# Attention followed by a SwiGLU feed-forward on one core: the first batch in a new order, other slots for the scores, no transposes in bare steps

## The chip, the cores and the metric

The kernel runs on one core of a Trainium2 chip. The metric is the device time of one execution in microseconds (us). Before the change the median of three runs is 423.39 us (423.31 to 423.66).

The engines of the core work at the same time, each through its own instructions in the order in which the program gives them: TensorE (PE: matmuls and transposes into PSUM; PEld is its loading of stationary operands), VectorE (DVE), ScalarE (ACT), GpSimd (POOL) and SyncE (SP, which here only issues DMAs). An instruction that waits holds up all that stands behind it on its engine. POOL issues DMAs too, those that change the type from fp32 to bf16 on the way among them.

## The reference

Eight batches, eight heads, 576 positions, head size 64. The attention has a causal mask and a decay that grows with the running sum of `max(s, 0)`:

```python
scores = scale * np.matmul(q, k.transpose(0, 1, 3, 2))
cum = np.cumsum(np.maximum(s, 0.0), axis=-1)
bias = -(cum[:, :, :, None] - cum[:, :, None, :])
scores = np.where(causal, -1000000000.0, scores + np.minimum(bias, 0.0))
attn = softmax(scores)                  # max subtracted, 1e-09 in the denominator
attn_out = np.matmul(attn, v)           # (8, 8, 576, 64)
x = attn_out.transpose(0, 2, 1, 3).reshape(4608, 512)
xn = x / rms(x) * rms_g
g = xn @ w_gate                         # 512 -> 1536
out = (g * sigmoid(g) * (xn @ w_val)) @ w_out
```

## The kernel before, in words

**The feed-forward is the frame.** The 4608 rows of x are cut into nine chunks of 512. `ffn(c)` does one chunk: for each of 12 blocks `fb` of the hidden size, four matmuls for the gate (line 482, called G here), four for the value (line 491, V), a tanh on ACT (485), two products on DVE (494 and 487); then 4 x 12 matmuls with `w_out` (line 506, O), four copies on ACT (511) and four stores by SP. `need(c)` comes before it and has to see that the rows of chunk c are there.

**The attention fills the frame.** After every group of four matmuls `ffn` calls `step()`, which counts a slot and puts a small piece of attention work into the program: 36 slots for each chunk. Its pieces are

- T (`t_step`, line 149): four transposes of k (w = 0) or q (w = 1) for one pair of heads, PSUM to `kqT` by ACT (161) or DVE (159); `tail_step` (163) for the last 64 positions.
- S (`s_step`, 188): for four heads and a block `kb` of 128 keys, score matmuls (203) into a pair of PSUM banks, four exps on ACT (219), and the causal mask by POOL (`affine_select`, 225). Half of the exps and the mask come one slot later (`pending`). In the frame the pair is always `psS`, of which there is one.
- AV (`av_step`, 233): E times V for four heads and 128 queries (240, 246), reciprocal and product on DVE (253, 255). With the second group of heads come a sum of squares on ACT (260) and the root on POOL (263, 266).
- `x_scale` (DVE, 273), XT (`xt_step`, 277: transposes on PE, 281, and a copy on DVE, 286, to `xnT`, which G and V read), `check_mag` and `check_max` (DVE), casts of k and q to bf16 (`cast`, 139 on POOL or DVE, 137 on ACT) and loads of V (`load_v`, 144, POOL).

Which piece a slot takes is fixed when the program is built, by rules in slots: S may follow S after three slots, or after two once the slot number has reached `due`:

```python
due = SLOTS * ((b * S + kb * 128) // DM) - 14
if slot[0] - last["S"] < (3 if slot[0] < due else 2):
```

XT may come six slots after the second AV of its block, `x_scale` three after it, T two slots after the last T or XT. `need(c)` calls `step()` with no matmuls of the frame around it while the last XT of its chunk is missing: bare steps. In the kernel before these are four ahead of chunk 1 and one ahead of chunk 2.

**The first batch comes ahead of the frame** and its order is written out by hand (lines 620 to 676), with `piece` for the casts and `s_first` for S. k and q of batch 0 come through SP in parts, k and q of batch 1 by four DMAs on POOL, and POOL also has the weights: `load_w` loads half of `w_gate` or `w_val` (`wg_sb`, `wv_sb`). All DMAs of POOL go through one queue (q0), those of SP through another (q1).

**PSUM** is eight banks: four in a ring named F (`psF`, `psF16`, `pairF` takes two), two for `psS`, one named AV (`psAV`, `psAV16`) and one named T (`psT`, `psT32`). In the frame F holds G, V and O.

Of the kernel before, what the change touches and what calls it, by code (L numbers as in the profile page):

```python
# [26 lines left out]
def kernel(  # L27
# [12 lines left out]
    nc = tc.nc  # L40
    B, H, S, D = q.shape
    DM = H * D
# [55 lines left out]
    def psF16():  # L98
        return pp.tile([128, 8, 128], BF16, name="psF16", tag="F", bufs=4)
# [7 lines left out]
    def psAV16():  # L107
        return pp.tile([128, 8, 128], BF16, name="psAV16", tag="AV", bufs=1)

    def psT():  # L110
        return pp.tile([128, 8, 128], BF16, name="psT", tag="T", bufs=1)
# [29 lines left out]
    def load_v(b, c):  # L141
        n = rows(c)
        done["V", b, c] = slot[0]
        nc.gpsimd.dma_start(  # L144
            out=v_sb[0:n, b % 2, c, :, 0:64],
            in_=v[b, :, c * 128:c * 128 + n, :].rearrange("h p d -> p h d"))
# [207 lines left out]
    def do_t(key, **kw):  # L354
        b, hp, w = key
        if hp == "tail":
            tail_step(b)
            done["T", b] = slot[0]
            after_tail(b)
        else:  # L360
            if b == 1 and (hp + w) % 2:
                kw["pT"] = psAV16()
            t_step(b, hp, w, **kw)
        done["T", b, hp, w] = slot[0]
        last["T"] = slot[0]
# [24 lines left out]
    def can_t():  # L390
        if not t_seq:
            return False
        b, hp, w = t_seq[0]
        if slot[0] - last["T"] < (1 if b == 1 else 2):
            return False
        return ready(2, "cast", b) and (b < 2 or ready(1, "S", b - 2, 4, 0))

    def can_s():
        if not s_seq or not slot_free():
            return False  # L400
        b, kb, g = s_seq[0]
        due = SLOTS * ((b * S + kb * 128) // DM) - 14
        if slot[0] - last["S"] < (3 if slot[0] < due else 2):
            return False
        if kb >= 3 and not ready(3, "T", b):
            return False
        if kb == 4:
            return True
        return all(ready(3, "T", b, 2 * g + j, w) for j in (0, 1) for w in (0, 1))
# [20 lines left out]
    scaled = [0]  # L430
    x_list = [(b, qb) for b in range(B) for qb in range(NSC)]

    def step():

        slot[0] += 1
        while pending:
            pending.pop(0)()
        if scaled[0] < len(x_list):
            b, qb = x_list[scaled[0]]
            if ready(3, "AV", b, qb, 1):  # L440
                x_scale(b, qb)
                scaled[0] += 1
        if v_side and (slot[0] % 2 or slot[0] < 9):
            run_side(v_side)
        else:
            run_side(pool_side)
        if slot[0] % 2:
            run_side(dve_side)
        if can_s():
            pending.append(do_s(s_seq.pop(0)))  # L450
            return
        n = 0
        if can_xt():
            do_xt(xt_seq.pop(0))
            n += 1
        if can_av():
            do_av(av_seq.pop(0))
            n += 1
        if n < 2 and can_t():
            do_t(t_seq.pop(0))  # L460

    def need(c):

        lastt = (c + 1) * DM - 1
        key = (lastt // S, (lastt % S) // 128)
        n = 0
        while at("XT", *key) > slot[0]:
            step()
            n += 1
            assert n < 200, key  # L470

# [44 lines left out]
    def load_w(src, dst, i):  # L516
        fs = slice(i * (DF // 2), (i + 1) * (DF // 2))
        nc.gpsimd.dma_start(out=dst[:, :, fs],
                            in_=src[:, fs].rearrange("(cc p) f -> p cc f", p=128))
# [62 lines left out]
    with tc.manual_schedule():  # L582

        nc.scalar.dma_start(out=s_sb, in_=s.rearrange("b h s -> (b h) s"))
        for g in (0, 1):
            for w in (0, 1):
                load_kq(nc.sync, 0, w, 4 * g, 4 * g + 4)
        nc.vector.memset(kq32[64:128, :, :, 256:320], 0.0)
        for w in (0, 1):
            load_kq_tail(nc.sync, 0, w)  # L590
        nc.sync.dma_start(out=g_row, in_=moe_rms_g.rearrange("(o d) -> o d", o=1).to_broadcast([128, DM]))
        make_identity(nc, ident_bf)
        make_identity(nc, ident_f)
        nc.gpsimd.memset(shf[:, 4, 64:128], 0.0)
        nc.gpsimd.memset(v_sb[:, 0, :, :, 64:65], 1.0)
        nc.gpsimd.memset(E[:, 6:8, :, 192:256], 0.0)
        nc.vector.memset(mhalf, -0.5)
        nc.vector.memset(stat, 0.0)
        nc.vector.memset(ss_all, 0.0)
        nc.vector.memset(acc, 0.0)  # L600
        nc.vector.memset(kqT[:, :, :, :, 576:640], 0.0)

        s_seq[:] = [x for x in s_seq if x[0] > 0 or x[1] == 4]
        av_seq[:] = [x for x in av_seq if x[0] > 0 or x[1] == 4]
        xt_seq[:] = [x for x in xt_seq if x[0] > 0 or x[1] == 4]
        t_seq[:] = [x for x in t_seq if x[0] > 0]
        scaled[0] = 4

        def piece(w, g, engines):
            for r, eng in enumerate(engines):  # L610
                cast(eng, 0, w, r, r + 1, 4 * g, 4 * g + 4)

        def pairF():
            return (psF(), psF())

        def s_first(kb, g, pair=None):
            return do_s((0, kb, g), pair)

        ACT, DVE, POOL = nc.scalar, nc.vector, nc.gpsimd
        piece(0, 0, (ACT, ACT, ACT, POOL))  # L620
        piece(1, 0, (ACT, ACT, POOL, POOL))
        load_v(0, 0)
        load_v(0, 1)
        do_t((0, 0, 0), pT=psT(), dve=False)
        do_t((0, 1, 0), pT=psF16(), dve=False)
        decay_setup()
        do_t((0, 0, 1), pT=psAV16(), dve=True)
        do_t((0, 1, 1), pT=psF16(), dve=True)
        s_first(0, 0)()
        piece(0, 1, (DVE, DVE, POOL, POOL))  # L630
        load_w(moe_w_gate, wg_sb, 0)
        piece(1, 1, (DVE, DVE, POOL, POOL))
        s_first(1, 0, pairF())()
        do_t((0, 2, 0), pT=psT(), dve=True)
        do_t((0, 3, 0), pT=psAV16(), dve=True)
        do_t((0, 2, 1), pT=psT(), dve=True)
        do_t((0, 3, 1), pT=psAV16(), dve=True)
        load_v(0, 2)
        s_first(0, 1, pairF())()
        s_first(1, 1)()  # L640
        load_w(moe_w_val, wv_sb, 0)
        do_av((0, 0, 0))
        do_av((0, 0, 1), psF())
        for w in (0, 1):
            cast(POOL, 0, w, 4, 5)
        s_first(2, 0, pairF())()
        tail_step(0)
        done["T", 0] = 0
        x_scale(0, 0)
        do_av((0, 1, 0))  # L650
        do_av((0, 1, 1), psF())
        load_v(0, 3)
        s_first(2, 1)()
        do_xt((0, 0))
        s_first(3, 0, pairF())()
        x_scale(0, 1)
        for w in (0, 1):
            load_kq(nc.gpsimd, 1, w)
            load_kq_tail(nc.gpsimd, 1, w)
        do_av((0, 2, 0))  # L660
        do_av((0, 2, 1), psF())
        s_first(3, 1)()
        do_xt((0, 1))
        x_scale(0, 2)
        do_av((0, 3, 0))
        do_av((0, 3, 1), psF())
        load_w(moe_w_gate, wg_sb, 1)
        load_w(moe_w_val, wv_sb, 1)
        do_xt((0, 2))
        nc.gpsimd.memset(v_sb[64:128, :, 4, :, 0:64], 0.0)  # L670
        nc.gpsimd.memset(v_sb[:, 1, :, :, 64:65], 1.0)
        x_scale(0, 3)
        check_mag(0, 0)
        check_mag(0, 1)
        done["check", 0] = 0
        do_xt((0, 3))
        for r in range(NSC):
            cast(ACT, 1, 0, r, r + 1)
            cast(POOL, 1, 1, r, r + 1)
        done["cast", 1] = -20  # L680
        for w in (0, 1):
            load_kq(nc.sync, 2, w)
            load_kq_tail(nc.sync, 2, w)
        done["raw", 2] = 5
        after_tail(0)
        later(v_side, 0, [
            lambda: load_v(0, 4), lambda: load_v(1, 0), lambda: load_v(1, 1),
            lambda: nc.gpsimd.dma_start(out=wout_sb,
                                        in_=moe_w_out.rearrange("(fc p) d -> p fc d", p=128)),
            lambda: load_v(1, 2), lambda: load_v(1, 3), lambda: load_v(1, 4)])  # L690
        check(0, True)
        check(1)

        def extra(fb):
            if fb == 8:
                decay_range()

        for c in range(NCH):
            need(c)
            ffn(c, extra if c == 0 else None)  # L700
            if c == B - 1:
                verdict()
# [185 lines left out]
```

## Time and profile before

| | us |
|---|---|
| median of three runs | 423.39 |
| the profiled execution | 423.98 |
| its span in the profile (first to last instruction) | 422.1 |
| first matmul of chunk 0 | 43.27 |
| first matmul of chunk 1 | 101.07 |

| engine | busy us | share of the span |
|---|---|---|
| PE | 373.4 | 88% |
| DVE | 300.1 | 71% |
| ACT | 242.0 | 57% |
| POOL | 174.9 | 41% |

How to read it: busy time of PE is a pipelined time and not a measure of speed by itself; "PEclk" is the clock that was granted to PE as a share of the full one. In the chain of waits, "A <- B: total, times, longest" says how long A stood idle until B released it. In the timeline a line has its start, its time, its engine, the line of the kernel, what was written from what, and in brackets the idle time before it with what ended it.

### The profile page before, as it was taken

What the parts mean: (1) busy time and instruction counts of PE and PEld (TensorE: products, weight loads), DVE (VectorE), ACT (ScalarE), POOL (GpSimd) and SP (SyncE); (2) the same over time, 40 slices, a digit from 0 to 9 for tenths busy, and PEclk for the clock granted to TensorE, in tenths of its full rate; (3) what the DMA queues carried; (4) which work ended last, traced back from release to release, by engine and by line L of the source; (5) the groups of instructions that cost most, each with busy time, mean ns of one, the idle gap of its engine ahead of it and who ended that gap; (6) DMA issues with size and microseconds to landing.
All of it is one profiled execution on the core that took longest, in us unless ns stands there. A gap on an engine that the chain in (4) does not pass through costs nothing. (4 is left out here: it accounts for less than half of the span.)

```text
span 422.1 us, 7394 instructions
## 1 busy us (share of the span) xinstructions
PE 373.4 (88%) x2679; PEld 182.6 (43%) x2679; DVE 300.1 (71%) x582; ACT 242.0 (57%) x600; POOL 174.9 (41%) x288
## 2 busy tenths in 40 slices
PE   2543888895998989999999999999999999999993
PEld 2222443353444444455444444544454445444441
DVE  5434678866798788887796888787757856774840
ACT  3565455772567758664867585758665873323321
POOL 5457736747417539635633582343220431000000
PEclk9999999896999999999999999999999999999999
DMA  8979999486930837729331630290020011001002
GB/s 236 121 94 233 215 232 174 26 240 107 156 103 1 242 90 51 222 81 82 113 114 75 64 20 0 77 79 5 10 91 2 0 52 52 0 26 76 0 28 80
DMA packets 69244, 38.71 MB, mean 92 GB/s; under 512 B 45904, under 2 KB 63824, under 8 KB 69200
## 3 DMA queue, kind: packets, MB, share of 16 engines
q0 software_dynamic: 41808, 11.80, 28.2%
q1 hardware_dynamic: 27312, 26.22, 20.7%
q8 instruction: 23, 0.38, 0.4%
q14 instruction: 21, 0.17, 0.1%
q10 hardware_dynamic: 80, 0.15, 0.1%
HBM read 38.16 MB, written 9.44 MB: 113 GB/s over the span
## 5 line engine op out<-in xcount | busy, mean ns | idle before, releaser
L219 ACT ACTIVATE E<-psS,biasK 128x256 bf16<-128x256 f32 (+2 forms) x304 | 106.8, 435 | 16.5 <-PE psS L203 16.4
L482 PE MATMUL psF<-xnT,wg_sb 128*128 128x512 bf16 x432 | 113.8, 387 | 2.7 <-DVE xnT L286 2.5
L491 PE MATMUL psF<-xnT,wv_sb 128*128 128x512 bf16 x432 | 113.7, 386 | 0.9 <-DVE Ht L487 0.9
L506 PE MATMUL psF<-wout_sb,Ht 128*128 128x512 bf16 x432 | 105.0, 380 | 0.0
L485 ACT ACTIVATE T<-psF 128x512 f32<-128x512 f32 x108 | 64.7, 599 | 60.9 <-PE psF L482 54.0
L225 POOL TENSOR_SCALAR_AFFINE_SELECT E<-E 128x512 bf16<-128x512 bf16 x72 | 54.0, 750 | 102.9 <-ACT E L219 102.7
L494 DVE SCALAR_TENSOR_TENSOR U<-T,psF 128x512 bf16<-128x512 f32 x108 | 73.8, 683 | 26.8 <-ACT T L485 26.2
L487 DVE TENSOR_TENSOR Ht<-U,psF 128x512 bf16<-128x512 bf16 x99 | 67.6, 682 | 5.5
L491 PEld LDWEIGHTS <-wv_sb 128*128 128x128 bf16 x432 | 39.4, 99 | 44.5 <-issue 7.5
L482 PEld LDWEIGHTS <-wg_sb 128*128 128x128 bf16 x432 | 38.7, 99 | 40.9 <-issue 10.1
L506 PEld LDWEIGHTS <-Ht 128*128 128x128 bf16 x432 | 37.7, 98 | 38.0 <-issue 2.8
L260 ACT ACTIVATE xs_sb<-x_sb 128x512 bf16<-128x512 bf16 (+1 forms) x40 | 25.2, 631 | 48.3 <-DVE x_sb L255 48.2
L139 POOL CAST kqn<-kq 128x512 bf16<-128x512 f32 (+1 forms) x74 | 47.3, 661 | 4.4 <-DMA kq<-in_k_dram 3.6
L273 DVE SCALAR_TENSOR_TENSOR xs_sb<-x_sb,al_all,g_row 128x512 bf16<-128x512 bf16 (+1 forms) x40 | 32.5, 812 | 15.9 <-POOL al_all L266 15.9
L511 ACT ACTIVATE osb<-psF 128x512 f32<-128x512 f32 x36 | 21.5, 598 | 27.4 <-PE psF L506 17.3
L263 POOL TENSOR_SCALAR al_all<-ss_all 128x1 f32<-128x1 f32 (+1 forms) x40 | 8.3, 207 | 66.3 <-ACT xs_sb L260 65.5
L144 POOL DMA_DIRECT2D v_sb<-in_v_dram x40 | 34.7, 872 | 0.9 <-issue 0.8
L255 DVE TENSOR_TENSOR x_sb<-psAV,rZ 128x256 bf16<-128x256 f32 (+1 forms) x76 | 32.1, 423 | 2.6
L153 PE MATMUL psT<-ident_bf,kqn 128*128 128x128 bf16 x220 | 23.2, 226 | 9.8 <-ACT kqn L137 6.8
L153 PEld LDWEIGHTS <-kqn 128*128 128x128 bf16 x256 | 19.9, 104 | 24.3 <-ACT kqn L137 7.2
L203 PE MATMUL psS<-kqT 64*128 64x256 bf16 (+2 forms) x304 | 26.3, 259 | 4.5 <-ACT E L219 3.9
L246 PEld LDWEIGHTS <-E 128*128 128x128 bf16 x320 | 22.9, 101 | 15.7 <-POOL E L225 7.6
(92 smaller groups left out, 330.0 us busy)
## 6 DMA issues: line engine op xcount, KB each, us to landing
out_dram<-osb SPq DMA_DIRECT2D x36, 256.0 KB, 2.0
kq<-in_k_dram SPq DMA_DIRECT2D x6, 1024.0 KB, 6.3
kq<-in_q_dram SPq DMA_DIRECT2D x6, 1024.0 KB, 7.4
v_sb<-in_v_dram POOLq DMA_DIRECT2D x32, 128.0 KB, 4.6
wg_sb<-in_moe_w_gate_dram POOLq DMA_DIRECT2D x2, 768.0 KB, 7.4
wv_sb<-in_moe_w_val_dram POOLq DMA_DIRECT2D x2, 768.0 KB, 9.7
wout_sb<-in_moe_w_out_dram POOLq DMA_DIRECT2D x1, 1536.0 KB, 18.1
kq<-in_k_dram SPq DMA_DIRECT2D x2, 512.0 KB, 6.2
```

What stands on the lines that cost most here:

```text
L139: eng.tensor_copy(out=o, in_=i)
L144: nc.gpsimd.dma_start(out=v_sb[0:n, b % 2, c, :, 0:64], in_=v[b, :, c * 128:c * 128 + n, :].rearrange("h p d -> p h d"))
L153: nc.tensor.matmul(pT[:, r, :], lhsT=kqn[:, b % 2, w, r, 2 * hp:2 * hp + 2, :], rhs=ident_bf, is_transpose=True, start=(r == 0), stop=(r = ...
L219: nc.scalar.activation(out=Ev[:, h - h0, 0:N], in_=pair[par][:, o:o + N], func=AF.Exp, scale=0.125, bias=biasK[:, kb, bh:bh + 1])
L225: nc.gpsimd.affine_select(out=Ev[:, :, 0:nq], in_=Ev[:, :, 0:nq], pattern=[[0, nh], [1, nq]], compare_op=ALU.is_ge, fill=0.0, base=0, chan ...
L273: nc.vector.scalar_tensor_tensor(out=xs_sb[0:n, (b * NSC + qb) % NX, :], in0=x_sb[0:n, (b * NSC + qb) % NX, :], scalar=al_all[0:n, col:col ...
L482: nc.tensor.matmul(Gp, lhsT=wg_sb[:, cc, fs], rhs=xnT[:, cc, x0:x0 + DM], start=(cc == 0), stop=(cc == CC - 1))
L485: nc.scalar.activation(out=T, in_=Gp, func=AF.Tanh, scale=0.5)
L487: nc.vector.tensor_tensor(out=Ht[:, fb - 1, :], in0=pend[0], in1=pend[1], op=ALU.mult)
L491: nc.tensor.matmul(Vp, lhsT=wv_sb[:, cc, fs], rhs=xnT[:, cc, x0:x0 + DM], start=(cc == 0), stop=(cc == CC - 1))
L494: nc.vector.scalar_tensor_tensor(out=U, in0=T, scalar=1.0, in1=Gp, op0=ALU.add, op1=ALU.mult)
L506: nc.tensor.matmul(Op, lhsT=Ht[:, fb, tb * 128:(tb + 1) * 128], rhs=wout_sb[:, fb, :], start=(fb == 0), stop=(fb == FB - 1))
```

## The change

It edits three rules of the frame and the order of the first batch.

1. In the frame `due` has 26 in place of 14, so that S may follow after two slots 12 slots earlier; T pieces of batch 1 with odd hp + w go to the ring F instead of bank AV; and bare steps take no T.
2. In the first batch POOL casts only a part of k and the two tails; ACT and DVE do the rest, ahead of the first S.
3. POOL's DMAs are issued at the start, as V0, V1, half of `w_gate`, V2, half of `w_val`, V3. The second half of `w_gate` follows before the fourth S, and the second half of `w_val` stays late. k and q of batch 1 go from POOL to SP, and to a much earlier place.
4. S is issued up to two units ahead of the AV that reads it; the second AV of each block takes bank T (`psT32`) instead of F; `x_scale` moves behind the first AV of the next block in most places; the last XT comes ahead of `check_mag`.
5. Two memsets of `v_sb` move from POOL behind the first batch to the start, one of them to DVE.

```diff
         else:
             if b == 1 and (hp + w) % 2:
-                kw["pT"] = psAV16()
+                kw["pT"] = psF16()
...
-        due = SLOTS * ((b * S + kb * 128) // DM) - 14
+        due = SLOTS * ((b * S + kb * 128) // DM) - 26
...
-    def step():
+    def step(bare=False):
...
-        if n < 2 and can_t():
+        if n < 2 and not bare and can_t():
             do_t(t_seq.pop(0))
...
         while at("XT", *key) > slot[0]:
-            step()
+            step(True)
...
-        nc.gpsimd.memset(v_sb[:, 0, :, :, 64:65], 1.0)
+        nc.gpsimd.memset(v_sb[:, :, :, :, 64:65], 1.0)
...
+        nc.vector.memset(v_sb[64:128, :, 4, :, 0:64], 0.0)
...
         piece(0, 0, (ACT, ACT, ACT, POOL))
-        piece(1, 0, (ACT, ACT, POOL, POOL))
+        piece(1, 0, (ACT, ACT, ACT, ACT))
         load_v(0, 0)
         load_v(0, 1)
+        load_w(moe_w_gate, wg_sb, 0)
+        load_v(0, 2)
+        load_w(moe_w_val, wv_sb, 0)
+        load_v(0, 3)
         do_t((0, 0, 0), pT=psT(), dve=False)
         do_t((0, 1, 0), pT=psF16(), dve=False)
         decay_setup()
         do_t((0, 0, 1), pT=psAV16(), dve=True)
         do_t((0, 1, 1), pT=psF16(), dve=True)
+        piece(0, 1, (DVE, DVE, DVE, DVE))
+        piece(1, 1, (DVE, DVE, ACT, ACT))
         s_first(0, 0)()
-        piece(0, 1, (DVE, DVE, POOL, POOL))
-        load_w(moe_w_gate, wg_sb, 0)
-        piece(1, 1, (DVE, DVE, POOL, POOL))
         s_first(1, 0, pairF())()
         do_t((0, 2, 0), pT=psT(), dve=True)
         do_t((0, 3, 0), pT=psAV16(), dve=True)
         do_t((0, 2, 1), pT=psT(), dve=True)
         do_t((0, 3, 1), pT=psAV16(), dve=True)
-        load_v(0, 2)
+        for w in (0, 1):
+            cast(POOL, 0, w, 4, 5)
+        load_w(moe_w_gate, wg_sb, 1)
+        for w in (0, 1):
+            load_kq(nc.sync, 1, w)
+            load_kq_tail(nc.sync, 1, w)
         s_first(0, 1, pairF())()
         s_first(1, 1)()
-        load_w(moe_w_val, wv_sb, 0)
         do_av((0, 0, 0))
-        do_av((0, 0, 1), psF())
-        for w in (0, 1):
-            cast(POOL, 0, w, 4, 5)
         s_first(2, 0, pairF())()
+        do_av((0, 0, 1), psT32())
+        s_first(2, 1, pairF())()
         tail_step(0)
         done["T", 0] = 0
+        do_av((0, 1, 0))
         x_scale(0, 0)
-        do_av((0, 1, 0))
-        do_av((0, 1, 1), psF())
-        load_v(0, 3)
-        s_first(2, 1)()
+        do_av((0, 1, 1), psT32())
         do_xt((0, 0))
-        s_first(3, 0, pairF())()
+        s_first(3, 0)()
+        do_av((0, 2, 0))
         x_scale(0, 1)
-        for w in (0, 1):
-            load_kq(nc.gpsimd, 1, w)
-            load_kq_tail(nc.gpsimd, 1, w)
-        do_av((0, 2, 0))
-        do_av((0, 2, 1), psF())
-        s_first(3, 1)()
+        do_av((0, 2, 1), psT32())
+        s_first(3, 1, pairF())()
         do_xt((0, 1))
+        do_av((0, 3, 0))
         x_scale(0, 2)
-        do_av((0, 3, 0))
-        do_av((0, 3, 1), psF())
-        load_w(moe_w_gate, wg_sb, 1)
+        do_av((0, 3, 1), psT32())
+        do_xt((0, 2))
         load_w(moe_w_val, wv_sb, 1)
-        do_xt((0, 2))
-        nc.gpsimd.memset(v_sb[64:128, :, 4, :, 0:64], 0.0)
-        nc.gpsimd.memset(v_sb[:, 1, :, :, 64:65], 1.0)
         x_scale(0, 3)
+        do_xt((0, 3))
         check_mag(0, 0)
         check_mag(0, 1)
         done["check", 0] = 0
-        do_xt((0, 3))
```

## The prediction

> **What bounds the kernel now.** I read the page, then the busy time by stretches cut at the gaps of PE, then the waits and the timeline around two of these gaps.
>
> ```profile
> span 422.1 us, 7394 instructions
> PE 373.4 (88%) x2679; PEld 182.6 (43%) x2679; DVE 300.1 (71%) x582; ACT 242.0 (57%) x600; POOL 174.9 (41%) x288
> ```
> ```profile
> core 0: us, PE busy (x) PEld busy (x) DVE busy (x) ACT busy (x) POOL busy (x), PEclk, DMA share, GB/s
> 0.00:43.27 43.27, 17.59 (x150) 10.75 (x151) 21.65 (x49) 21.34 (x54) 24.97 (x49) 1.00 0.89 169
> ...
> 50.00:77.40 27.40, 22.45 (x155) 10.19 (x153) 22.94 (x47) 16.81 (x45) 14.75 (x19) 0.96 1.57 183
> ...
> 95.60:101.07 5.47, 1.22 (x16) 0.98 (x17) 4.23 (x10) 1.80 (x4) 3.33 (x6) 0.82 0.37 133
> 101.07:108.10 7.03, 7.03 (x28) 3.01 (x27) 4.29 (x8) 1.19 (x2) 5.50 (x7) 0.65 0.86 92
> ...
> 160.00:400.00 240.00, 237.22 (x1707) 115.12 (x1705) 181.93 (x355) 147.34 (x363) 85.01 (x142) 1.00 0.29 56
> ```
>
> From 160 to 400 us PE is busy 237.2 of 240: there it is the bound, and the change removes none of its work. What can be gained lies ahead: 43.27 us to the first G, gaps in chunk 0, and the boundary to chunk 1 (95.60 to 101.07, PE busy 1.22), after which PE runs at a mean clock of 0.65 for 7.03 us.
>
> The waits of the first batch, and three lines of its end:
>
> ```profile
> PE psF L246 <- POOL E L225: 7.1, 3, 2.8
> DVE xs_sb L273 <- POOL al_all L266: 5.7, 3, 2.9
> ACT E L219 <- PE psF L203: 3.5, 1, 3.5
> ```
> ```profile
> 34.91 0.70 POOL L129 DMA_DIRECT2D kq<-in_q_dram  x1
> ...
> 36.55 1.12 DVE L273 SCALAR_TENSOR_TENSOR xs_sb<-x_sb,al_all,g_row 128x512 bf16<-128x512 bf16 x1 [2.92 <-POOL al_all L266]
> ...
> 43.27 1.86 PE L482 MATMUL psF<-xnT,wg_sb 128*128 128x512 bf16 x4 [1.38 <-DVE xnT L286]
> ```
>
> POOL's queue is the knot: its casts hold back the transposes, its masks the AVs, and DMA issues of 0.7 to 0.9 us stand ahead of the root. No engine is busy more than 25 of 43 us. At the boundary:
>
> ```profile
> 96.65 0.39 PE L153 MATMUL psT<-ident_bf,kqn 128*128 128x128 bf16 x4
> 99.97 0.58 PE L281 MATMUL psT<-ident_bf,xs_sb 128*128 128x128 bf16 x4 [2.94 <-ACT kqT L161]
> 101.07 1.86 PE L482 MATMUL psF<-xnT,wg_sb 128*128 128x512 bf16 x4 [0.52 <-DVE xnT L286]
> ```
>
> A T in a bare step took bank T; its copy stood on ACT behind a sum of squares, and the XT for which chunk 1 waits came 2.94 us late.
>
> **The first batch, by compute.** I carry it forward with the durations of its rows. q's four casts on ACT (0.36 each) end at 8.97 and their transposes still follow decay_setup at 9.66, so the first S stays at 12.09 on ACT. Its two added casts (10.85 to 11.6) fit ahead. DVE has six casts instead of four (0.22 each): done at 12.85 instead of 12.4. But nothing waits for POOL any more, whose last cast ran to 16.54. The four copies of T on DVE begin at 13.15 instead of 15.44, and the exps of S(0,1) at 16.4 instead of 18.66. From there ACT is the chain: eight S of 1.57 or 1.37, squares of 0.82, one tail copy: S(2,1) ends at 23.2; then the tail's copy on ACT, and DVE's behind it (23.75), with the product of AV(1,0) queued on DVE, and XT and the second AVs taking turns in bank T: each use is freed by DVE (19.7, 23.75, 25.6, 26.65, 29.5) before ACT runs dry for more than 0.2, apart from 2.2 us ahead of the square of AV(1); S(3,1) ends at 31.7. Its mask is done at 32.35; AV (0.8), product (0.55), square (0.8), root (0.9), x_scale (0.75), XT and copy (1.4) follow, and G begins at 37.75: 5.5 us earlier. POOL's six DMA issues (0.8 to 1.0 each) run from 6.85 to 12.4, under the wait for the first exps (its mask starts at 13.73). If they took 2 us longer, the first AV would still not be late: it comes at 17. The memset on DVE (0.9, by L588) lies in an idle time of 1.99, the longer one on POOL before 6.36. With the latter two gone from 42.30, POOL's casts of batch 1 follow the root 1.8 us sooner; nothing waited for them there.
>
> **The first batch, by DMA.** V3 is needed at 30.1 for AV(3,0). The transfers of batch 0 keep the engines until about 15 both before and after, V0 and V1 (landing at 14.3 and 15.2) included. A half weight is 5.0 us of all 16 engines (62.9% of 24 to 32 us). A V is 2.25: q0's 28.2% of 422 us is 119; less 4 halves, w_out as two, and k and q of batch 1 at q1's rate (20.7% of 422 for 26.2 MB, so 7.9), 81 us remain for 36 full V. Ahead of V3's end in q0 are now two halves and two V: 14.5 us, so 29.5. But k and q of batch 1 now come through SP from 12.5 on, another 7.9: between 29.5 and 37.4. Shared queues are in the trace:
>
> ```profile
> wv_sb<-in_moe_w_val_dram POOLq DMA_DIRECT2D x1, 768.0 KB, 6.9
> ```
> ```profile
> wv_sb<-in_moe_w_val_dram POOLq DMA_DIRECT2D x1, 768.0 KB, 12.5
> ```
>
> The first was issued at 22.34 alone, the second at 41.23 behind a half weight and beside k and q of batch 2: both queues advance together. I take 34.0, nearer to the shared end. From V3 to the first G are 6.5 us (37.02 to 43.27 before, plus waits): G at 40.5, **2.8 us earlier**. The Trainium skill speaks against the move here (DMA: Bandwidth & Descriptors, "Queues, rings and completion order"): each engine goes round-robin between queue rows by packets, so V3 would share until k and q are done, 37.4 at worst and G 0.6 later than now; in strict order of issue V3 would land at 29.5 and the 5.5 stand.
>
> **Slots 1 to 12.** The plan, followed slot by slot, is the same as before. T of batch 1 in F instead of AV takes away the wait of 1.51 us of PE for x_sb (57.91); it shortens the ring for G and V, which then wait for the product two steps back: 0 to 1 us, I take 0.5, by the waits for Ht of 0.7 that exist. **-1.0.**
>
> **Slots 13 to 24.** S of batch 1 comes at 13, 15, 17, 19, 21, 23 instead of 13, 16, 19, 22, 24, and two more AVs fall here. DVE is busy 22.9 of 27.4 us, so they count in full, at 0.59: **+1.2** (0 if it has room).
>
> **Boundary to chunk 1.** The last S of batch 1 comes at 28 instead of 31, the AV on which XT(1,3) hangs at 31 instead of 34, and XT at 37 behind one bare step instead of at 40 behind four; that step takes no T. Five groups of O cover the chain. The 5.47 us become XT 0.4, copy and start 0.5, some wait 0.3; but T and AV (0.75) that ran in the gap now run elsewhere: **-3.5**. With no long gap the clock need not fall: 0.35 of 7.03 us, **-2.5**. The Trainium skill (TensorE: Matmul & The Clock Gate, Part 1) has the clock halve after an idle window of about 3.4 us; no single wait here was above 2.94, and the clock fell all the same, so I go by the sum of idle time: by its rule nothing would be lost now and the 2.5 would have to be something else.
>
> **Later chunks.** Two bare steps instead of one ahead of chunk 2, since chunk 1 starts three slots sooner and its XT only two: a slot, 36 to a chunk of 39 us, **+1.0**. S two slots after S: 16 times instead of 7. psS is one, so each waits for the exps before it: waits of PE for them are 0.3 to 0.7; 9 times 0 to 0.37, half taken: **+1.5**.
>
> **Sum:** -2.8 - 1.0 + 1.2 - 3.5 - 2.5 + 1.0 + 1.5 = -7.1. The profiled 423.98 (span 422.1 and 1.9 around it) becomes 416.9, the median of 423.39 becomes **416.3**.
>
> **Rivals.** (1) Compute alone bounds the first batch and close S cost nothing: -5.5 for -2.8, 0 for 1.5, so 412.1. For it: chain on ACT without stalls; against: the DMA engines have no pause. (2) V3 lands last of all, at 37.4: G at 43.9, +3.4, so 419.7. For it: the landing of 12.5; against: q1 gets all of its share only if SP issues in time, and the q load waits for POOL's tail casts near 17. (3) The rules of the frame don't do what they say: XT(1,3) is late for another reason and the clock falls; 3.5 and 2.5 are missing, 422.3. (4) Slower: close S make ACT the bound. In two slots (2.17 us at 39 us a chunk) it would have four exps (1.74), a tanh (0.60), a square (0.82), at times a copy of T (0.59): 3.2 to 3.75, so 1.0 to 1.6 for each of nine added close S, with T, G and V queued on PE behind the S that waits. At 1.3 that is 11.7 instead of 1.5: 426.5. It decides from 1.05 each. Against: ACT is busy 57%, not every pair has a square, and the seven close S now show no wait above 0.7.
>
> **How the numbers follow.** Forecast 0.62, its own range 412.5 to 419.5 (V3 between 31 and 36; the DVE term 0; the clock loss kept). Rival 1 0.08, rival 2 0.12, rival 3 0.07, rival 4 0.11. The range is 411.5 to 422.3: it leaves out rival 4 and thin tails. A measurement here tells 0.2%, 0.85 us, from no change. Faster 0.86 (forecast and rivals 1 to 2, most of 3), same 0.03, slower 0.11.
>
> **What would show it.** First G near 40.5 in the timeline, with AV(3,0) waiting for a DMA if I am right about V3, and for the mask otherwise; no wait of XT for a copy of T ahead of chunk 1, its first G near 95, clock 1.00 behind it. Waits of PE on psS for exps that sum to some 2 us more; with 8 more, rival 4 holds. A first G after 43 with a wait for V is rival 2.

## The result: 0.3% slower, with the gains of the first batch and of chunk 1 spent by chunk 4

Side by side on one chip the changed kernel took 425.01 us (median of 20 runs, 423.5 to 426.96), the kernel before 423.51 (20 runs). The ratio is 1.0032, with a 95% interval of 1.0018 to 1.0046. The profiled execution of the changed kernel took 426.65 (span 425.0), 1.6 above its median; this kernel's runs spread over 3.5 us, so lines of one profile are good to about that much in the sum, and much better for a single wait.

The page of the changed kernel:

```profile
span 425.0 us, 7348 instructions
PE 371.9 (88%) x2631; PEld 182.8 (43%) x2679; DVE 305.1 (72%) x585; ACT 243.0 (57%) x604; POOL 168.5 (40%) x276
```

Some 48 matmul records are missing from it, so counts of PE are a little low. DVE has 5 us more than before, POOL 6 less.

The end of the first batch, from the timeline:

```profile
32.45 0.21 PE L246 MATMUL psAV<-v_sb,E 128*128 128x65 bf16 x1 [2.75 <-DMA v_sb<-in_v_dram]
...
38.93 0.58 PE L482 MATMUL psF<-xnT,wg_sb 128*128 128x512 bf16 x1 [0.52 <-DVE xnT L286]
```

AV(3,0) waits 2.75 us for V3, and the first G comes 4.34 us earlier than before (38.93 for 43.27). The boundary to chunk 1 is short as well; the 2.94 us of XT behind a T have become 0.28:

```profile
92.33 0.38 PE L281 MATMUL psT<-ident_bf,xs_sb 128*128 128x128 bf16 x4 [0.28 <-DVE kqT L159]
...
93.40 0.81 PE L482 MATMUL psF<-xnT,wg_sb 128*128 128x512 bf16 x3 [0.68 <-DVE xnT L286]
```

Chunk 1 so begins 7.67 us earlier (93.40 for 101.07), and yet the end is later. Two places give most of it back. One is inside chunk 0; first the kernel before, then the changed one:

```profile
72.09 0.40 ACT L545 ACTIVATE s_sb<-cum,rng 64x128 f32<-64x128 f32 x1 [3.52 <-DVE rng L543]
...
74.75 0.20 PE L240 MATMUL psAV<-v_sb,E 128*128 128x65 bf16 x1 [1.74 <-DVE x_sb L255]
```
```profile
66.91 0.40 ACT L545 ACTIVATE s_sb<-cum,rng 64x128 f32<-64x128 f32 x1 [3.57 <-DVE rng L543]
...
68.69 0.81 ACT L219 ACTIVATE E<-psS,biasK 128x256 bf16<-128x256 f32 x2
...
69.55 0.61 PE L203 MATMUL psS<-kqT 64*128 64x256 bf16 x4 [3.84 <-ACT E L219]
```

`decay_range` puts three exps on ACT, the first of which waits 3.57 us for DVE. In the kernel before it waited as long (3.52), and an AV of PE 1.74 us. In the new plan an S stands in the same slot: half of its exps come behind these, and the next S waits 3.84 us for the one `psS`, all of PE's queue behind it. The clock falls around it:

```profile
65.70:70.33 4.63, 0.79 (x6) 0.29 (x6) 2.94 (x13) 3.11 (x10) 0.75 (x2) 0.78 0.25 14
70.33:77.15 6.82, 6.82 (x40) 2.61 (x38) 6.34 (x11) 4.45 (x13) 5.66 (x9) 0.65 0.47 31
```

(Stretch and its length, then busy us of PE, PEld, DVE, ACT and POOL, the granted clock, DMA.) The clock no longer falls at the boundary to chunk 1, but the profile has as much low clock as before, in other places: half the full clock from 75.3 to 78.7 and from 99.2 to 106.0 us before, from 68.3 to 75.1 and from 177.5 to 181.0 now, 10.2 us in both up to the last copy. The other place is chunk 2. One stretch of it from the timeline, DVE's queue and the AV that waits for it:

```profile
172.06 0.69 DVE L494 SCALAR_TENSOR_TENSOR U<-T,psF 128x512 bf16<-128x512 f32 x1 [0.68 <-ACT T L485]
...
172.85 0.69 DVE L501 TENSOR_TENSOR Ht<-U,psF 128x512 bf16<-128x512 bf16 x1
173.45 0.82 DVE L291 TENSOR_SCALAR mag<-kqn 128x2560 uint16<-128x2560 uint16 x1
...
174.19 1.14 DVE L273 SCALAR_TENSOR_TENSOR xs_sb<-x_sb,al_all,g_row 128x512 bf16<-128x512 bf16 x1
...
175.25 0.17 DVE L253 RECIPROCAL rZ<-psAV 128x4 f32<-128x4 f32 x1
175.45 0.42 DVE L255 TENSOR_TENSOR x_sb<-psAV,rZ 128x256 bf16<-128x256 f32 x1
...
175.93 0.20 PE L240 MATMUL psAV<-v_sb,E 128*128 128x65 bf16 x1 [1.95 <-DVE x_sb L255]
```

ACT gives the tanh late, DVE's product waits 0.68, and behind it stand the last product, a check and an `x_scale`, then the reciprocal and the product that free bank AV. The waits of PE over the whole run, for the kernel before and for the changed one:

```profile
PE psS L203 <- ACT E L219: 3.9, 9, 0.7
...
PE psT L281 <- DVE kqT L159: 1.3, 1, 1.3
```
```profile
PE psS L203 <- ACT E L219: 5.5, 5, 3.8
PE psT L281 <- DVE kqT L159: 3.8, 5, 1.2
...
PE psAV L240 <- DVE x_sb L255: 3.4, 4, 2.0
```

XT behind a T in bank T waits five times instead of once for DVE's copy.

The place of the loss is easiest read from the length of the chunks. I take the start of ACT's last copy (line 511) of each chunk from the timelines, and the first G for the start; us:

| kernel | first G | chunk 0 | 1 | 2 | 3 | 4 | 5 | 6 | 7 and 8 |
|---|---|---|---|---|---|---|---|---|---|
| before | 43.3 | 54.0 | 48.3 | 45.1 | 40.7 | 42.3 | 40.4 | 38.6 | 63.0 |
| changed | 38.9 | 57.3 | 41.8 | 50.2 | 43.1 | 42.7 | 40.3 | 39.8 | 62.9 |
| changed, due 14 | 38.9 | 52.4 | 46.9 | 44.1 | 40.4 | 41.8 | 40.4 | 38.6 | 63.0 |
| before with due 26 alone | 43.3 | 57.6 | 42.1 | 50.0 | 43.1 | 42.7 | 40.3 | 39.7 | 62.9 |
| changed, `decay_range` in chunk 7 | 39.0 | 53.6 | 42.0 | 48.8 | 43.1 | 42.7 | 40.3 | 39.4 | 63.8 |
| due 26, no checks | 38.4 | 49.5 | 38.5 | 44.6 | 41.4 | 40.3 | 40.3 | 39.4 | 62.9 |
| due 14, no checks | 38.8 | 48.5 | 42.7 | 42.8 | 40.0 | 41.1 | 40.4 | 38.6 | 63.0 |

Against before, the changed kernel gains 4.4 ahead of chunk 0 and 6.5 in chunk 1; it loses 3.3 in chunk 0, 5.1 in chunk 2, 2.4 in chunk 3, 0.4 in chunk 4 and 1.2 in chunk 6. Some 1.4 of the loss in chunk 2 is its stretch of low clock, which is missing from the 48.8 of the kernel with `decay_range` in chunk 7.

The table ends at the last copy, where the two profiles are 1.4 us apart; the other 1.5 of their 2.9 us lie behind it. From the start of the last copy to the end the kernel before takes 6.48 us, the changed one 7.95. The trace shows where: the first two DRAIN instructions of SP at the end of the program (line 883 before, 882 now) start 5.58 and 5.65 us after that copy before, 5.52 and 7.00 now. The distance is 0.06 and 0.07 us in the two profiles with the old first batch, whose SP has 157 instructions, and 1.2 to 1.8 us in all sixteen with the new one, whose SP has 165. So the new first batch also costs some 1.4 us at the very end, about as much as the whole measured difference; why the drain comes late was not tried.

### The profile page after: what moved, and what is told of

It reads as the page before. It is cut to its first block, busy times and chain, and to the rows that moved or that the text cites. A ratio compares the mean times of both kernels' runs of the same rounds, so it can differ in the third digit from the quotient of the medians.

```text
span 425.0 us, 7348 instructions
## 1 busy us (share of the span) xinstructions
PE 371.9 (88%) x2631; PEld 182.8 (43%) x2679; DVE 305.1 (72%) x585; ACT 243.0 (57%) x604; POOL 168.5 (40%) x276
## 5 line engine op out<-in xcount | busy, mean ns | idle before, releaser
L482 PE MATMUL psF<-xnT,wg_sb 128*128 128x512 bf16 x412 | 111.2, 385 | 3.8 <-DVE xnT L286 2.4
L491 PE MATMUL psF<-xnT,wv_sb 128*128 128x512 bf16 x421 | 112.1, 385 | 2.3 <-DVE Ht L487 1.1
L219 ACT ACTIVATE E<-psS,biasK 128x256 bf16<-128x256 f32 (+2 forms) x300 | 105.2, 436 | 10.1 <-PE psS L203 9.7
L506 PE MATMUL psF<-wout_sb,Ht 128*128 128x512 bf16 x415 | 101.5, 382 | 0.8
L491 PEld LDWEIGHTS <-wv_sb 128*128 128x128 bf16 x432 | 38.5, 99 | 45.5 <-issue 10.0
L482 PEld LDWEIGHTS <-wg_sb 128*128 128x128 bf16 x432 | 38.8, 99 | 41.4 <-issue 8.3
L506 PEld LDWEIGHTS <-Ht 128*128 128x128 bf16 x432 | 39.0, 98 | 40.9 <-issue 2.3
L139 POOL CAST kqn<-kq 128x512 bf16<-128x512 f32 (+1 forms) x68 | 44.9, 679 | 3.6 <-DMA kq<-in_k_dram 3.6
L273 DVE SCALAR_TENSOR_TENSOR xs_sb<-x_sb,al_all,g_row 128x512 bf16<-128x512 bf16 (+1 forms) x40 | 34.7, 868 | 8.4 <-POOL al_all L266 8.4
L263 POOL TENSOR_SCALAR al_all<-ss_all 128x1 f32<-128x1 f32 (+1 forms) x40 | 9.4, 236 | 69.5 <-ACT xs_sb L260 69.0
L246 PE MATMUL psAV<-v_sb,E 128*128 128x65 bf16 x304 | 28.4, 197 | 2.7 <-DMA v_sb<-in_v_dram 2.7
L286 DVE COPY xnT<-psT 128x512 bf16<-128x512 bf16 (+1 forms) x40 | 15.5, 387 | 18.8 <-PE psT L281 18.8
```

The costliest lines, as they stand in the source:

```text
L139: eng.tensor_copy(out=o, in_=i)
L219: nc.scalar.activation(out=Ev[:, h - h0, 0:N], in_=pair[par][:, o:o + N], func=AF.Exp, scale=0.125, bias=biasK[:, kb, bh:bh + 1])
L273: nc.vector.scalar_tensor_tensor(out=xs_sb[0:n, (b * NSC + qb) % NX, :], in0=x_sb[0:n, (b * NSC + qb) % NX, :], scalar=al_all[0:n, col:col ...
L482: nc.tensor.matmul(Gp, lhsT=wg_sb[:, cc, fs], rhs=xnT[:, cc, x0:x0 + DM], start=(cc == 0), stop=(cc == CC - 1))
L491: nc.tensor.matmul(Vp, lhsT=wv_sb[:, cc, fs], rhs=xnT[:, cc, x0:x0 + DM], start=(cc == 0), stop=(cc == CC - 1))
L506: nc.tensor.matmul(Op, lhsT=Ht[:, fb, tb * 128:(tb + 1) * 128], rhs=wout_sb[:, fb, :], start=(fb == 0), stop=(fb == FB - 1))
```

## The experiments

The medians below stand against runs of the kernel before on the same chip, whose medians were 423.77, 423.69, 423.36 and 423.76 in the four groups.

### One part at a time

**The new order of the first batch alone**, with all three rules of the frame as before:

```diff
-        due = SLOTS * ((b * S + kb * 128) // DM) - 26
+        due = SLOTS * ((b * S + kb * 128) // DM) - 14
-                kw["pT"] = psF16()
+                kw["pT"] = psAV16()
-        if n < 2 and not bare and can_t():
+        if n < 2 and can_t():
```

> The new order of the first batch alone, with the rules of the frame as before (due 14, transposes of batch 1 in bank AV, transposes allowed in bare steps). Theory A (the first batch's gain is real and stays; what ate it is the rule due - 26): first G of chunk 0 near 38.9 as in the changed kernel, and 4.3 us less at the end, 419 to 420. Rival B (the gain of the first batch is given back in the later chunks whatever the rules, because the attention's chain on DVE and ACT sets their pace): first G near 38.9 too, but 422.5 to 424 at the end.

Measured: 420.16, ratio 0.9919 (0.9899 to 0.9938); first G at 38.80. Most of the gain of the first batch stays: chunks 1 to 6 are as long as before, within 0.9, and of the 4.5 us at the first G (38.80 for 43.27) 3.6 are left at the end, behind the later drain of SP.

**due 26 alone**, in the kernel before:

```diff
-        due = SLOTS * ((b * S + kb * 128) // DM) - 14
+        due = SLOTS * ((b * S + kb * 128) // DM) - 26
```

> The kernel before with due 26 instead of 14 and nothing else. Theory A: slower, 425 to 429: the boundary to chunk 1 loses its bare steps (-3 to -4), but the S of slot 17 stands across the exps of decay_range (+3.8, and 3 for the clock), and later chunks lose some 7 to collisions of XT and AV with T on DVE. Rival B: 423 to 424.5, since what is moved earlier only waits elsewhere. Rival C (the ban on T in bare steps is what costs): 419 to 422, since due alone takes bare steps away.

Measured: 429.33, ratio 1.0124 (1.0105 to 1.0143). The rule alone costs 5.6 us, with the same 3.83 us of wait at `decay_range`, and chunks of 50.0, 43.1 and 42.7 us for 2 to 4: the lengths of the changed kernel, within 0.2. So these belong to the rule, not to the first batch. Chunk 1, counted with its boundary, gets 6.2 us shorter (42.1 for 48.3); chunk 0 and chunks 2 to 6 get 12.3 longer.

**The changed kernel with due 14:**

```diff
-        due = SLOTS * ((b * S + kb * 128) // DM) - 26
+        due = SLOTS * ((b * S + kb * 128) // DM) - 14
```

> The changed kernel with due back at 14. Theory A: 417 to 420, a gain of 5 to 8 on the changed kernel: the first batch's 4.3 and the 2.9 of XT behind a T at the boundary stay, and the later collisions go. Rival B: 423 to 425. Rival C: 424 to 426, as the changed kernel.

Measured: 415.54, ratio 0.9834 (0.9802 to 0.9865): below what was expected. One number makes 9.5 us of 425.0 by the medians, and 8.4 by the ratios: two of these six runs took 418.7, the others 415.2 to 415.6, and the median passes over the two.

**T allowed in bare steps again**, at due 14:

```diff
-        if n < 2 and not bare and can_t():
+        if n < 2 and can_t():
```

> The changed kernel with due 14 and with transposes allowed again in bare steps: the first batch and the ring F for T remain. If XT behind a T in bank T at the boundary costs what the trace of before shows (2.94 us, and a longer cold clock behind the gap), this is 3 to 4 us slower than the changed kernel with due 14 (415.5): 418 to 420. If the ban is worth nothing (the T then only stands elsewhere), 415 to 416.5.

Measured: 420.03, ratio 0.9915 (0.9899 to 0.993). At due 14 the ban is worth 4.5 us by the medians (3.4 by the ratios). The wait of 2.9 us of XT for ACT's copy is back in it. But hardly any of the gain lies at the boundary: with the ban G of chunk 1 still waits 2.36 us for `xnT`, and between the two profiles chunk 1, counted with its boundary, differs by 0.1, chunks 0, 2, 3 and 4 by 1.3, 1.0, 0.3 and 0.5. Against the first run of this section this kernel differs only by T in the ring F, which so is worth 0.1 us, not clear of noise.

Put on one after the other, -3.6 (first batch), -0.1 (F), -4.5 (ban) and +9.5 (due) make +1.3; the measured difference is +1.5. That they add up shows nothing, since each of these kernels is one edit from the next. And the last two edits are not independent. With due 26 no T falls into a bare step even where it may: followed slot by slot, the kernel before with due 26 alone has the same bare steps as the changed kernel, one ahead of chunk 1 and two ahead of chunk 2, none with a T, and PE's weight loads come in the same order in both traces from the first G on. So at due 26 the ban does nothing. By itself due 26 costs 5.6; in the changed kernel it leaves 1.5 + 3.6 + 0.1 = 5.2, and the rest of the 9.5 is the gain that the ban has at due 14 and loses.

### The first batch and V3

V3 issued ahead of the half of `w_val`, at due 14:

```diff
-        load_w(moe_w_val, wv_sb, 0)
         load_v(0, 3)
+        load_w(moe_w_val, wv_sb, 0)
```

> The changed kernel with due 14, and V3 issued ahead of the half of w_val instead of behind it. If V3's landing (32.45 in the changed kernel, with AV(3) waiting 2.75 us for it) is what sets the end of the first batch, V3 lands near 27 and the first G comes at 37.0 to 37.8 instead of 38.9: 1.0 to 1.8 us less, 413.7 to 414.6. If the mask of S(3,1) sets it anyway, no change: 415.5.

Measured: 413.53, ratio 0.9777 (0.9756 to 0.9797), 2.0 us less than without the swap, a little more than expected. V3 now lands at 27.14 instead of 32.41 and the half of `w_val` at 32.43 instead of 28.34: what stands first in POOL's queue lands first. The timeline shows the wait for V gone and the mask in its place:

```profile
31.93 0.24 PE L246 MATMUL psT<-v_sb,E 128*128 128x65 bf16 x1 [1.61 <-POOL E L225]
...
37.21 0.59 PE L482 MATMUL psF<-xnT,wg_sb 128*128 128x512 bf16 x1 [0.52 <-DVE xnT L286]
```

### decay_range

```diff
-            ffn(c, extra if c == 0 else None)
+            ffn(c, extra if c == 7 else None)
```

In the changed kernel:

> The changed kernel with decay_range (three exps on ACT with a chain to DVE, in chunk 0 so far) moved to chunk 7, where no attention is left. Theory A in its part on decay_range: the wait of 3.84 us of PE on psS near 65.7 goes, and the cold clock of 6.83 us behind it: 419 to 421.5. Rival B: the time is given back by chunk 2: 424 to 425.

Measured: 422.71, ratio 0.9973 (0.9956 to 0.9991), 2.3 us under the changed kernel. The wait of 3.84 is gone, waits of 0.56 and 1.42 stand near its place, and the mean granted clock of the run is 0.997 instead of 0.982. Chunk 0 is 3.7 shorter and chunk 2 1.4, but the run does not reach the 419 to 421.5 that was expected. In its new place the helper costs 0.9 (chunks 7 and 8 take 63.8 for 62.9), so by an estimate from these numbers its collision with S is worth some 3.2.

### Why due 26 costs so much behind chunk 0

The expectations below call two explanations Theory D (DVE's load) and Theory E (the order of the slots). **The checks left out**, at due 26 and at due 14 (the range test of the inputs is then not done; the slots of all S, AV, T and XT stay the same):

```diff
     def check(b, started=False):
+        done["check", b] = slot[0]
+        return
```

> The changed kernel (due 26) without check_mag and check_max of the frame: six instructions of 0.82 us on DVE for each batch are left out, so the range test of the inputs is not done. Theory D (due 26 loses because it puts more of the attention's DVE work into the slots of G and V, where DVE already has two products of 0.68 for each block, so that XT and AV wait for copies and products queued on DVE): most of the loss goes with the load, and the distance to the same kernel with due 14 falls from 9.5 to 2 to 5 us; 413 to 418. Theory E (the loss is in the order of the slots itself, through ACT or the banks, not in DVE's load): the distance stays at 8 to 10; 420 to 424.

> The partner of the run before: due 14, and check_mag and check_max of the frame left out. Theory D and E: 411 to 414.5 (waits for DVE in chunk 0 sum to some 4 us, part of them goes). Only its distance to the run with due 26 counts.

Measured: 406.31, ratio 0.9595 (0.9579 to 0.961), at due 26, and 405.00, ratio 0.9538 (0.9519 to 0.9557), at due 14. The distance falls from 9.5 to 1.3 (some 3 between those runs of the two whose mean granted clock was 0.995 or more). The collision at `decay_range` shrinks with it: its exps no longer wait for DVE at due 26, and S waits 1.52 us for `psS` instead of 3.84. The same chunk 2 in the four kernels (busy us of PE, PEld, DVE, ACT, POOL): changed; due 14; due 26 without checks; due 14 without checks.

```profile
138.00:188.30 50.30, 44.46 (x356) 22.51 (x359) 41.95 (x85) 31.32 (x81) 27.12 (x43) 0.97 0.60 127
```
```profile
138.20:182.20 44.00, 42.15 (x352) 21.38 (x349) 39.22 (x80) 31.05 (x79) 24.52 (x39) 1.00 0.57 122
```
```profile
126.40:171.00 44.60, 42.53 (x356) 21.86 (x359) 32.91 (x73) 31.21 (x81) 25.32 (x44) 1.00 0.65 143
```
```profile
130.00:172.80 42.80, 41.78 (x347) 21.32 (x350) 31.70 (x69) 31.09 (x79) 22.58 (x40) 1.00 0.59 126
```

With due 26 the chunk holds 2.7 us more of DVE's work (41.95 for 39.22) and is 6.3 longer, its low clock included; without the checks, DVE at 32.9 of 44.6, it is only 1.8 longer. ACT has the same 31 us in all four.

**The checks in the slots of O only**, with all work done, at due 26:

```diff
-        if slot[0] % 2:
+        if phase[0]:                       # 1 while ffn is in its matmuls with w_out
             run_side(dve_side)
```

> The changed kernel (due 26) with all its work, but check_mag and check_max of the frame run in the slots of O, where DVE has no products, instead of in odd slots of the whole chunk. The order of S, AV, T and XT is that of the changed kernel, slot by slot. Theory D: most of what leaving the checks out gave (425.0 to 406.3) comes, 408 to 414. Theory E (leaving the checks out helped because there was less work, wherever it stood): 420 to 425.

Measured: 421.47, ratio 0.9932 (0.9908 to 0.9957). Only 3.5 us, far from the 408 to 414 that was expected. Chunk 0 is 4.8 shorter (52.5 for 57.3). Chunks 3 and 4 get shorter (41.7 and 40.7 for 43.1 and 42.7), but chunk 1 gets longer (45.3 for 41.8) and chunk 2 stays at 50.0. AV waits 3.19 us for x_sb near the end of chunk 0; that a check in each slot of O makes a new heap there is my reading of it, not shown apart.

**The copies of T of q on ACT**, from batch 2 on, and **the checks in every fourth slot** instead of every second, both with all work done:

```diff
+            if b > 1:
+                kw["dve"] = False
             t_step(b, hp, w, **kw)
```

> The changed kernel (due 26) with all its work, but the copies of T of q (w = 1) run on ACT instead of DVE from batch 2 on: 0.59 on ACT for 0.69 on DVE, four for each batch. Theory D' (DVE's queue is what XT and AV wait for, through the single banks T and AV, wherever the load stands): the waits of XT for L159 on DVE go, the wait of AV for x_sb near 176 shrinks, and chunks 2 to 4 (50.2, 43.1, 42.7) get 3 to 6 shorter together: 419 to 422. Theory E (ACT or the order): chunks 2 to 4 stay or grow, 424 to 427.

Measured: 421.14, ratio 0.9922 (0.9896 to 0.9948). Chunks 2 and 3 are 2.0 and 1.1 shorter than in the changed kernel, chunk 4 is the same: 3.1 of the 3 to 6 expected, but some 1.4 of it is the low clock in chunk 2, which this profile lacks. The AV that waited 1.95 us waits 1.36.

```diff
-        if slot[0] % 2:
+        if slot[0] % 4 == 1:
             run_side(dve_side)
```

> The changed kernel (due 26) with all its work, check_mag and check_max spread over every fourth slot instead of every second one; the order of S, AV, T and XT and the loads is the same slot by slot. If pile-ups of DVE (a check in the same slots as AV, x_scale and the products) are what counts, and moving the checks to the 12 slots of O only piled them up there: 415 to 420. If it is the sum of DVE's work over chunks 0 to 4: 423 to 425.

Measured: 421.94, ratio 0.9951 (0.9931 to 0.9971), 3.1 under the changed kernel: between the two theories. Each of three ways to relieve DVE's crowded slots is worth 3 to 4 us; none brings the 9.5 back.

**due 18:**

```diff
-        due = SLOTS * ((b * S + kb * 128) // DM) - 26
+        due = SLOTS * ((b * S + kb * 128) // DM) - 18
```

> The changed kernel with due 18, between 14 (415.5) and 26 (425.0). The plan's DVE work of the attention in the slots of G and V of chunk 2 is 12.5 us with 14, 14.3 with 18, 15.2 with 26, and an S stands next to decay_range only with 26 (slot 17). Theory D: in between, 417 to 421, with chunk 2 some 2 to 4 us longer than with 14. If only the S at decay_range counts: 415 to 416.5.

Measured: 416.14, ratio 0.9818 (0.9791 to 0.9845), with 14's 415.54 within the intervals. Theory D asked for more. But the reading "only the S at `decay_range` counts" fails too: here an S stands behind it as well and PE waits longer than in the changed kernel,

```profile
70.78 0.61 PE L203 MATMUL psS<-kqT 64*128 64x256 bf16 x4 [4.25 <-ACT E L219]
```

while chunk 1 (42.5) keeps most of the gain of earlier S and chunks 2 to 4 (45.9, 40.7, 41.4) are 1.8, 0.3 and -0.4 longer than with 14. The loss behind chunk 0 is not in proportion to the slots; it sets in between 18 and 26.

### Versions that beat both kernels

The changed kernel with due 14, V3 first, `decay_range` in chunk 7 and the checks in the slots of O; then the same with due 26:

> What the runs point to, together: the changed kernel with due 14, V3 ahead of the half of w_val, decay_range in chunk 7, and the checks in the slots of O. 413.5 less some 1 to 2 for decay_range and 2 to 6 for the checks: 406 to 411.

> As the run before, but with due 26: whether the early scores pay once DVE is free of the checks beside G and V. Without the checks the two were 1.3 apart in favour of 14. 407 to 412; Theory D leaves at most 3 us between this and its partner.

Measured: 415.55, ratio 0.9804 (0.9759 to 0.9848), and 417.33, ratio 0.9854 (0.9827 to 0.9881). The first is no better than due 14 by itself: the checks in the slots of O take back what V3 and `decay_range` give (chunks 1 and 2 are 48.1 and 47.8 instead of 46.9 and 44.1). So the 1.8 us between the two, within the 3 expected, do not show that due 26 has become cheap: the move spoils the kernel with due 14. Without that move, at due 14 and at due 18:

> The changed kernel with due 14, V3 ahead of the half of w_val and decay_range in chunk 7; the checks where they were. 413.5 less 1 to 3 (a wait of AV of 1.74 us at decay_range and the cold clock behind it): 410.5 to 412.5.

> The same with due 18, where the S of slot 18 stood behind decay_range and cost 4.24 us: 416.1 less 2.0 for V3 and 3 to 4.5 for decay_range: 409.5 to 411.5, below its partner with 14 if the bare steps that it saves count.

Measured: 411.50, ratio 0.9701 (0.9671 to 0.9731), and **411.11, ratio 0.9693 (0.9668 to 0.9717)**, 3% under the kernel before. The two can't be told apart. With due 18 the profile shows no low clock between the first chunk and the end, and chunk 2 is 1.8 us longer than with 14 (45.9 for 44.1).

## Why the prediction was wrong

**The sum.** The seven terms add up to -6.1 and not to the -7.1 that the prediction gives, so its terms forecast 417.3 instead of 416.3, and each rival that swaps terms comes out 1.0 higher. The last term is mis-worked too: half of nine times 0.37 is 1.7, not 1.5. Neither decides anything here.

**First batch: right in kind, 2.8 forecast for 4.3 at the first G and 3.6 at the end.** The carried timeline stood: exps of S(0,1) at 16.53 (16.4 forecast), the mask of S(3,1) done at 31.7 (32.35). V3 was in use from 32.45, where I had taken 34.0 between 29.5 and 37.4, and the first G came at 38.93 for 40.5. That V3's place behind the half of `w_val` in POOL's queue sets the end is shown by the swap, which took 2.0 us off. How much of the wait is k and q of batch 1, which by the Trainium skill (DMA: Bandwidth & Descriptors, "Queues, rings and completion order") share the engines in a round-robin, was not tried; 32.45 lies between the 29.5 of strict order and the 37.4 of equal shares in the prediction. SP's late drain, 1.4 us, was in no term.

**Slots 1 to 12: -1.0 forecast, 0.1 measured** for T in F. The wait of 1.51 us at 57.9 went. Between the two profiles that differ by F alone, at due 14, 3.4 us of low clock stand in chunk 0 instead of at the boundary.

**Boundary: -6.0 forecast, and it came.** The first G of chunk 1 is at 93.40 (95 forecast) with no low clock behind it, and chunk 1 with its boundary is 6.5 us shorter, 6.2 by due alone. The ban, which I booked inside this term, has no part in it. It is worth 4.5 at due 14, little of it at the boundary; why there is not shown. For the -2.5 of the clock I took the low clock as bound to this gap. The profile has as much of it as before, behind the 3.84 us in chunk 0 and behind the 1.95 us in chunk 2.

**The failed step is the price of due 26 outside the boundary:** +1.2 for two AVs in chunk 0, +1.0 for a bare step and +1.5 for nine close S, 3.7 together. In the kernel before, with due 26 alone, chunks 0 and 2 to 6 are 12.3 us longer, so that the rule, forecast to save 2.3 with its boundary, costs 5.6. I priced close S by the waits of PE on `psS` in the kernel before, of at most 0.7 us. Two things were not in that row. First, the plan put an S into the slot of `decay_range`, which I had followed slot by slot without asking which exps would stand behind it on ACT: 3.84 us, and with the clock 2.3 by the move of `decay_range`. Second, the S that come earlier bring their AV, `x_scale` and XT with them, into slots in which DVE had little room; I counted DVE's load only for chunk 0 and not for chunk 2, where it is at 38.7 of 45.1 us in the kernel before. XT and AV then wait for banks T and AV that DVE frees late. That DVE's load is what makes due 26 dear is shown by the pair without checks (1.3 for 9.5), the collision at `decay_range` included, whose exps wait for DVE. Against ACT's load speak its equal 31 us in chunk 2 and the run that moved copies from DVE to ACT and got faster; ACT's order was not tested apart. It is not shown which pieces meet: relieving DVE's crowded slots gave 3 to 4 us in each of three ways, and due 18 gave nearly all. That stays open.

**Rival 4** had the sign, the place in the queue of S and nearly the time (426.5), but not the mechanism: it made ACT the bound everywhere, and outside chunk 0 the waits on `psS` sum to less than before (1.7 us for 2.9).

## What to carry to other kernels

A rule that lets work come earlier moves all that follows from it too: count the load of every engine in the slots to which it goes, chunk by chunk, not only the wait that the moved instruction had before. Before shifting a schedule by a few slots, look what other work with a chain between two in-order engines stands at the new place; here one helper that runs once made PE wait 3.84 us. And when several edits come together, time each alone and ask whether one leaves another anything to do: at due 14 the first batch and the ban are worth 8 us together, due 26 alone costs 5.6, and with due 26 the ban has nothing left to ban.

## What the runs showed of the hardware

At due 14 the granted clock fell around waits of 0.81 and 2.36 us at the boundary to chunk 1 (0.51 from 92.8 to 99.7), as in the kernel before around 0.81 and 2.94. Each of these waits is shorter than the idle window of about 3.4 us after which the Trainium skill has the clock fall (TensorE: Matmul & The Clock Gate, Part 1). The length of one wait does not decide it either: the same AV waits 1.95 us in chunk 2 of the changed kernel and of the one with `decay_range` in chunk 7, and the clock falls behind it in the first (0.51 from 177.5 to 181.0) and not in the second, whose mean clock is 0.997. What decides was not found. A V of 128 KB issued at 11.24 landed 21.2 us later with two half weights and three V issued ahead of it on POOL still under way and k and q of the next batch beside it, against 3.8 us in the kernel before, where it was issued at 29.94 with nothing ahead of it in POOL's queue.
